# Six places for low parts and four for loads in a Fourier-mixing and attention kernel, with the space taken from the big matrix, and copies that either engine may do

## The chip, the core and the metric

The kernel runs on one core of a Trainium2 chip. The metric is the device time of one execution in microseconds (us): the median of several runs. Beside it one execution is recorded by the hardware profiler; its span is counted from the first instruction to the last.

The core has five engines that matter here: TensorE (PE; its weight loads are listed apart as PEld), ScalarE (ACT), VectorE (DVE), GpSimd (POOL) and SyncE (SP). All transfers between memory and the on-chip buffers are issued from SP's queue. Matrix products go to eight banks of PSUM, from which only ACT and DVE can read here.

## The reference: what is computed

Two independent parts, whose outputs lie side by side (2048 rows of 448 + 448).

```python
# part A: Fourier mixing, S = 2048, D = 448
a = einsum("bsd,ed->bse", x, dft_hid_re);  b = einsum("bsd,ed->bse", x, dft_hid_im)
y = einsum("ts,bse->bte", dft_seq_re, a) - einsum("ts,bse->bte", dft_seq_im, b)
# part B: attention, 16 heads of 28
q, k, v = split(x @ wqkv)
p = softmax(q @ k.T * 28**-0.5);  o = (p @ v) @ wo
out = concatenate([y, o], axis=-1)
```

All is float32. A matrix product that must be precise is made of products of two parts: each operand is split into a high part (rounded to the matmul's format, F32R) and a low part (what is left), and high x high, low x high and high x low are added up in PSUM.

## The kernel before

**A planner writes the order.** The kernel is not written in the order in which it runs. Every piece of work is a task: an engine (or a choice of two, with a price on each), a key, the tasks it depends on, and the buffers it uses. `Schedule.run` (L192) then plays the five engines against each other with the prices given and writes the instructions out: an engine that comes free takes the ready task with the smallest key. A task is ready when its dependencies are done and each buffer it needs has a free place. The result is a fixed order on each engine. So a change of a price, a key or a number of places changes the order of everything behind it.

**Buffers are pools with places** (`Slots`, L100). A place is taken when the first task that uses it is written, and given back when the last one is done. Pools marked "in turn" give their places out in the order of keys. The pools that matter:

- `wraw` (3 places): raw loads, of weights, of folded input rows, and of one in four tiles of the sequence matrix.
- `whi` (3) and `wlo` (4): their high and low parts; `wlo` also holds the differences of three in four sequence tiles.
- `kept` (19 pairs of 512 columns): results on their way out, loads of input rows, intermediate sums, and the exponentials of the attention. A pair for exponentials is only given if one more stays free (`SPARE`).
- `big`: one large tile whose ranges are reused by stage (input of the projections; then the hidden stage's results, the low parts of its tables at 7 S, and at its end, from `TAIL`, the last quarter of the late projection).

**Two streams share TensorE.** One is the attention: for each head and each four key tiles, 16 score matmuls (L1196), 16 exponentials on ACT (L1200), then 32 matmuls for the weighted sum (L1207), which need all 16. The other, called fill, runs in this order:

1. projections of q, k and v (`project`, `values`; matmuls at L573). Their results are split by ACT (L614) and DVE (L615) and stored.
2. the hidden stage of part A, folded by symmetry. `weights_both` adds and subtracts halves of the hidden matrix (L753) and writes tables from the four results (L758 to L766); the tables wait until the projections 1 to 4 are stored, since they lie where those were staged. `rows_both` loads eight pairs of input row tiles (L780), `folded` adds and subtracts their halves into `wraw` (L789), takes half of that as the high part (L791) and the rest as the low part (L792); the matmuls are at L816.
3. the sequence stage, twice (real and imaginary part): `combine` loads and adds the hidden results (L846 to L856), `sequence_halved` loads the sequence matrix (L949), splits a quarter of it (L956, L957), takes differences of the other tiles (L986 to L997) and their largest value (L939), and multiplies (L967).
4. the late projection of the attention's output (`project_late`): three of the four row blocks as soon as heads 0 to 13 are done (loads L1409, splits L1415 and L1417, matmuls L1430), the last block of rows at the end (load L1448, splits L1450 and L1451, two matmuls for each of 16 row groups at L1461). Twelve groups are held on chip in between and added (L1465); the last four stay in their banks and are copied by ACT (L1469) and sent (L1470).

**Keys.** Scores have keys from `T_ATT` to `T_END`, evenly spread over the heads; fill has keys that grow with the planned matmul time, up to `T_FILL`; the last block has `T_OUT` and on. The first keys of a group of heads (`tops`, L1160), from which the rows subtracted before the exponential come, run `LEAD` = 24 ahead of the group's first score. After each head the sums are normalised through memory (`normal`, L1254): copy, store, load, reciprocal, store, load, multiply, store.

## Time and profile before

| | us |
|---|---|
| median of 3 runs | 832.52 (831.48 to 832.91) |
| the profiled execution, its own time | 827.46 |
| its span | 825.6 |
| TensorE busy | 807.9 |
| ACT busy | 619.2 |
| DVE busy | 399.6 |

A row of the groups gives line, engine, operation, what is written from what, the shapes and how many; then busy time in us, the mean of one in ns, and the idle time of the engine just before them with what ended it. Rows of the chain of waits and of the timeline begin with the start and the length in us; "x32" means 32 instructions merged. Buffer names leave out the number of the place. The tile called `wdraw` lies in the same memory as `wd`.

### The profile page before, as it was taken

The numbers are of one execution on the slowest core, as the hardware profiler recorded it, in microseconds if no ns is written. First come the engines' busy times: TensorE is split into PE (matmuls) and PEld (weight loads), VectorE is DVE, ScalarE is ACT, GpSimd is POOL, SyncE is SP. The second block draws the span as 40 slices with busy tenths as digits, with TensorE's granted clock in tenths as the row PEclk, the third lists the DMA queues.
The fourth block names the chain that finished last, engine by engine and source line by source line (L and its number), as shares of the span: only waits on it lengthen the run. The fifth ranks groups of instructions, "written<-read, shape, count | busy, mean of one in ns | idle before, by whom it ended". The sixth has DMA issues, their size and how long they took to land.

```text
span 825.6 us, 14220 instructions
## 1 busy us (share of the span) xinstructions
PE 807.9 (98%) x4872; PEld 524.5 (64%) x4872; DVE 399.6 (48%) x925; ACT 619.2 (75%) x1274; POOL 7.9 (1%) x58
## 2 busy tenths in 40 slices
PE   8999999999999999999999999999999999999994
PEld 7886555755666666657665677656765666655574
DVE  6541324342332335357655378976754476533142
ACT  6207886677888889998777687999777768889731
POOL 3000000000000000000000000000000000000000
PEclk9999999999999999999999999999999999999997
DMA  8747766534423245577646267678766456560143
GB/s 292 229 148 258 213 205 207 200 104 155 133 94 121 74 155 175 174 163 233 207 150 205 69 196 240 209 197 245 218 199 214 143 164 213 156 203 14 34 128 109
DMA packets 136048, 141.28 MB, mean 171 GB/s; under 512 B 36830, under 2 KB 106976, under 8 KB 135968
## 3 DMA queue, kind: packets, MB, share of 16 engines
q1 hardware_dynamic: 135968, 140.29, 55.1%
q8 instruction: 40, 0.66, 0.3%
q14 instruction: 40, 0.33, 0.1%
HBM read 98.82 MB, written 43.12 MB: 172 GB/s over the span
## 4 chain that ended last, share of the span: by engine, by line
PE 93%; DMA 2%; ACT 2%; SPq 1%; DVE 0%; issue 0%; ACTq 0%
PE bank L1196 31%; PE bank L1207 27%; PE bank L573 13%; PE bank L967 12%; PE bank L816 5%; PE bank L1430 3%; ACT kept L1200 1%; PE bank L915 1%; PE bank L1180 1%; DMA kept<-xb 1%; DMA wraw<-wim 1%; DMA kept<-abd 1%; PE bank L1461 1%; PE bank L1287 0%; DMA kept<-ond 0%
## 5 line engine op out<-in xcount | busy, mean ns | idle before, releaser
L1200 ACT ACTIVATE kept<-bank 128x512 f32<-128x512 f32 x1024 | 510.7, 673 | 107.0 <-PE bank L1196 106.2
L1196 PE MATMUL bank<-q,k 85*128 85x512 f32 x1024 | 374.4, 413 | 3.6 <-ACT kept L1200 3.6
L1196 PEld LDWEIGHTS bank<-q,k 85*128 85x128 f32 x1024 | 186.5, 189 | 100.5 <-issue 39.0
L1207 PE MATMUL bank<-kept,v 128*32 128x512 f32 x2048 | 233.9, 597 | 0.0
L1207 PEld LDWEIGHTS bank<-kept,v 128*32 128x32 f32 x2048 | 60.6, 110 | 130.8 <-issue 124.3
L967 PE MATMUL bank<-big,wlo 128*128 128x226 f32 x512 | 106.6, 277 | 0.0
L967 PEld LDWEIGHTS bank<-big,wlo 128*128 128x128 f32 x512 | 96.3, 198 | 9.5 <-issue 0.7
L967 PE MATMUL bank<-big,whi 128*128 128x448 f32 (+1 forms) x256 | 74.6, 323 | 0.0
L573 PE MATMUL bank<-big,whi 128*128 128x512 f32 x196 | 69.6, 398 | 2.3 <-ACT big L512 1.4
L939 DVE TENSOR_REDUCE diff<-wlo 128x1 f32<-128x512 f32 x96 | 65.5, 683 | 2.5
L967 PEld LDWEIGHTS bank<-big,whi 128*128 128x128 f32 x256 | 49.6, 198 | 5.0 <-ACT kept L1200 0.5
L439 DVE COPY kept<-bank 128x226 f32<-128x226 f32 (+4 forms) x63 | 30.3, 502 | 42.5 <-PE bank L816 39.0
L573 PEld LDWEIGHTS bank<-big,whi 128*128 128x128 f32 x196 | 36.8, 189 | 12.5 <-ACT big L512 1.8
L573 PE MATMUL bank<-big,wlo 128*128 128x512 f32 x112 | 44.4, 398 | 0.0
L957 DVE TENSOR_TENSOR wlo<-wraw,whi 128x512 fp32r<-128x512 f32 x32 | 22.0, 688 | 45.2 <-PE bank L967 33.4
L816 PE MATMUL bank<-wd,whi 128*128 128x450 f32 (+3 forms) x128 | 42.7, 369 | 0.0
L573 PE MATMUL bank<-wd,big 128*128 128x448 f32 x176 | 37.6, 370 | 0.0
L1430 PE MATMUL bank<-big 128*128 128x448 f32 x144 | 37.1, 366 | 0.0
L573 PEld LDWEIGHTS bank<-wd,big 128*128 128x128 f32 x176 | 32.8, 188 | 3.9 <-issue 0.7
L986 DVE TENSOR_TENSOR wlo<-wdraw,wraw 128x256 fp32r<-128x256 f32 x64 | 24.4, 423 | 21.5 <-PE bank L967 7.2
L615 DVE TENSOR_TENSOR wd<-bank,wd 128x512 fp32r<-128x512 f32 x16 | 10.8, 686 | 45.4 <-ACT wd L614 43.4
L1260 ACT ACTIVATE kept<-bank 128x512 f32<-128x512 f32 (+1 forms) x19 | 11.5, 606 | 24.0 <-PE bank L1207 24.0
(119 smaller groups left out, 616.9 us busy)
## 6 DMA issues: line engine op xcount, KB each, us to landing
wdraw<-wre SPq DMA_DIRECT2D x48, 256.0 KB
wdraw<-wim SPq DMA_DIRECT2D x48, 256.0 KB
qkd<-wd SPq DMA_DIRECT2D x32, 256.0 KB
q<-qkd SPq DMA_DIRECT2D x64, 112.0 KB
k<-qkd SPq DMA_DIRECT2D x64, 112.0 KB
abd<-kept SPq DMA_DIRECT2D x16, 448.0 KB
kept<-abd SPq DMA_DIRECT2D x16, 448.0 KB
qkd<-kept SPq DMA_DIRECT2D x24, 256.0 KB
```

Of the source, the lines that this page charges most:

```text
L439: nc.vector.tensor_copy(dst, src)
L573: nc.tensor.matmul(o.t[:, :cols], w(), x(), start=(i == 0), stop=(i == n - 1))
L816: nc.tensor.matmul(o.t[:, c0:c1], of(w, i), y(), start=n == 0, stop=n == m)
L939: seen.append(dve(key, lambda: nc.vector.tensor_reduce(dst, f32(flat(src.t)), axis=AX.X, op=ALU.max, apply_absolute_value=True), 0.6, deps ...
L957: b = dve_on(key - 11.5, lambda e: e.tensor_tensor(turned(lo.t), read(same.t), f32(turned(hi.t)), op=ALU.subtract), 0.65, deps=[a], acq=[l ...
L967: nc.tensor.matmul(o.t[:, at0:at0 + n], cut_of(w.t, e, c), x(), start=first, stop=stop)
L986: e.tensor_tensor(turned(dl.t, c, 2, HP), read(r.t, c, 2, HP), read(base.t, c, 2, HP), op=op)
L1196: m = pe(key, lambda e: nc.tensor.matmul(b.t, KT[h][kt // 4].t[:KR + 1, kt % 4 * P:(kt % 4 + 1) * P], q.t[:KR + 1, :], start=True, stop=True),
L1200: return act(key - 20, lambda: nc.scalar.activation(p.t, b.t, AF.Exp, scale=SCALE), deps=[m], use=[b, pair])
L1207: nc.tensor.matmul(o.t[j * VW:(j + 1) * VW, :], VT[h].t[:, kt // 4, kt % 4, :], tiles[i // 2].t[:, i % 2, :], start=(kt < 4 // len(cs)), s ...
L1260: a = act(key - 20, lambda: nc.scalar.activation(osb.t[:n * VW], o.t[:n * VW], AF.Copy, accum_out=sums[:n * VW, g:g + 1]), deps=[dep], use ...
L1430: nc.tensor.matmul(o.t[:, :D], a(), b(), start=(i == 0), stop=(i == 8 and n < N_HELD))
```

## The change

- `wraw` gets a fourth place, `wlo` two more (six). `big` loses 1688 columns behind `TAIL`.
- The low parts of the hidden tables (`low_at`) are no longer in `big`: they take two places of `wlo` for as long as the hidden stage runs.
- The last quarter of the late projection keeps its three high parts in the three places of `whi`, not in `big`.
- Three kinds of copy that only ACT did may be done by ACT or DVE, whichever the planner finds free: the high part of a projection's result (L614), half of the folded rows (L791, "first half"), and the copies of the last four output groups (L1469).
- Each of the last four output groups waits for the end of its own chain of matmuls instead of the end of the last chain.
- Four numbers of the plan: `T_ATT` 24 to 26, `T_END` 666 to 610, `T_FILL` 867 to 926, `T_OUT` 788 to 806.

```diff
-    big = new("big", [P, TAIL + 1736], F32R)
+    big = new("big", [P, TAIL + 48], F32R)
-    wraw = new("wraw", [P, 4, P], F32, 3, True)
+    wraw = new("wraw", [P, 4, P], F32, 4, True)
-    wlo = new("wlo", [P, 4, P], F32R, 4, True)
+    wlo = new("wlo", [P, 4, P], F32R, 6, True)
...
-    T_ATT, T_END, T_FILL, T_OUT = 24.0, 666.0, 867.0, 788.0
+    T_ATT, T_END, T_FILL, T_OUT = 26.0, 610.0, 926.0, 806.0
...
-            a = act(key, lambda o=o, hi=hi: nc.scalar.activation(as_r(hi.t), o.t, AF.Copy), deps=[end], use=[o, *own])
+            a = sch.add({"ACT": ACT_P, "DVE": DVE_P}, key, lambda e, o=o, hi=hi: copy_of(e, as_r(hi.t), o.t), deps=[end], use=[o, *own])
...
-    low_at = [big[:, 7 * S + i * EVEN:7 * S + i * EVEN + (EVEN if i < 2 else ODD)] for i in range(4)]
+    low_in = [wlo.slot() for _ in range(2)]
+
+    def low_at(i):
+        n = EVEN if i < 2 else ODD
+        return flat(low_in[i // 2].t)[:ROWS[i % 2], i % 2 * n:(i % 2 + 1) * n]
...
-        h = act(key + 1, lambda: nc.scalar.activation(hi.t, raw.t, AF.Copy, scale=0.5), ACT_S, deps=d, acq=[hi], use=[raw])
+        def half_of(e):
+            if e == "ACT":
+                nc.scalar.activation(hi.t, raw.t, AF.Copy, scale=0.5)
+            else:
+                nc.vector.tensor_scalar(hi.t, raw.t, 0.5, None, op0=ALU.mult)
+        h = sch.add({"ACT": ACT_S, "DVE": 0.6}, key + 1, half_of, deps=d, acq=[hi], use=[raw])
...
-    mid = [big[:, TAIL + 3 * CH + i * 3 * HT:TAIL + 3 * CH + (i + 1) * 3 * HT] for i in range(2)]
+    mid = [big[:, TAIL + i * 3 * HT:TAIL + (i + 1) * 3 * HT] for i in range(2)]
...
+        last_in = [whi.slot() for _ in range(3)]
+        at_last = lambda c, *ks: [last_in[k] for k in ks if c == 3 and k < 3]
...
         def place_of(c, k):
-            at = 2 * GROUP * (c + 1) + k * CH
-            if c == 3:
-                at = TAIL + k * CH if k < 3 else 2 * GROUP * (k - 2) + 6 * CH
+            if c == 3 and k < 3:
+                return flat(last_in[k].t)
+            at = 2 * GROUP * (c + 1) + k * CH if c < 3 else 2 * GROUP * (k - 2) + 6 * CH
             return big[:, at:at + CH]
...
-                held[n] = o
+                held[n] = o, last[0]
...
-            p = pe(key, emit, n=2, d=M448, deps=[x3_ready[c], *w_ready, *([] if n < N_HELD else [last[0]])], use=[o, x3[c]])
+            p = pe(key, emit, n=2, d=M448, deps=[x3_ready[c], *w_ready, *([] if n < N_HELD else [held[n][1]])], use=[o, x3[c]])
...
-                e = act(key, lambda o=o, pair=pair: nc.scalar.activation(pair.t[:, 0, :D], o.t[:, :D], AF.Copy), 0.43, deps=[p], use=[o, pair])
+                e = sch.add({"ACT": 0.43, "DVE": 0.53}, key, lambda e, o=o, pair=pair: copy_of(e, pair.t[:, 0, :D], o.t[:, :D]), deps=[p], use=[o, pair])
```

More of the change, by code (lines that the diff above doesn't have):

```diff
@@ L760, in weights_both @@
                 ts.append(dve(at, lambda i=i, n=n, pick=pick: nc.vector.tensor_tensor(
-                    halves(low_at[i][:n]), pick(i // 2), halves(f32(table(i, "hi"))), op=ALU.subtract), 0.35, deps=[ts[i // 2]], use=[to]))
+                    halves(low_at(i)), pick(i // 2), halves(f32(table(i, "hi"))), op=ALU.subtract), 0.35, deps=[ts[i // 2]], use=[to, low_in[i // 2]]))
                 for a, op2 in ((0, ALU.subtract), (1, ALU.add)):
@@ L808, in hidden_both @@
                     seq += [(hi, i, lambda i=i: table(i, "main"), 0, 2 * MAIN, M448), (lo, i, lambda i=i: table(i, "hi"), c0, c1, MLOW),
-                            (hi, i, lambda i=i: low_at[i][:ROWS[i % 2]], c0, c1, MLOW)]
+                            (hi, i, lambda i=i: low_at(i), c0, c1, MLOW)]
                 rest = [(hi, i, lambda i=i: table(i, "rest"), 0, 2 * REST, M448) for i in range(4)]
@@ L817, in hidden_both @@
                         last[0] = pe(at, emit, d=d, deps=[last[0], *([h, *ready] if n == 0 else [l] if n == 1 else [])],
-                                     use=[hi, lo, o, *([pair] if n == len(seq) - 1 else [])])
+                                     use=[hi, lo, o, *low_in, *([pair] if n == len(seq) - 1 else [])])
                         at += d
@@ L1415, in project_late @@
                     a = act(key + 2 + i * 36 * M448, lambda raw=raw, i=i, c=c, k=k: nc.scalar.activation(place_of(c, k), raw.t[:, i], AF.Copy), ACT_S,
-                            deps=[ld, free], use=[raw])
+                            deps=[ld, free], use=[raw, *at_last(c, k)])
                     b = dve_on(key + 2 + i * 36 * M448, lambda e, raw=raw, i=i, c=c, k=k: e.tensor_tensor(
-                        place_of(c, 3 + k), raw.t[:, i], f32(place_of(c, k)), op=ALU.subtract), 0.62, deps=[a], use=[raw])
+                        place_of(c, 3 + k), raw.t[:, i], f32(place_of(c, k)), op=ALU.subtract), 0.62, deps=[a], use=[raw, *at_last(c, k)])
                     x[c, k] = [a, b]
@@ L1430, in emit @@
                     nc.tensor.matmul(o.t[:, :D], a(), b(), start=(i == 0), stop=(i == 8 and n < N_HELD))
-                last[0] = pe(key + i * M448, emit, d=M448, deps=[last[0], *x[c, i // 3], *(w_ready if i == 0 else ())], use=[o])
+                last[0] = pe(key + i * M448, emit, d=M448, deps=[last[0], *x[c, i // 3], *(w_ready if i == 0 else ())], use=[o, *at_last(c, 0, 1, 2)])
             if n < N_HELD:
@@ L1456, in project_late @@
             key = T_OUT + n
-            o = bank_s.slot() if n < N_HELD else held[n]
+            o = bank_s.slot() if n < N_HELD else held[n][0]
             def emit(e, n=n, o=o, xt=x3[c], t=t):
```

## The prediction

> **What bounds the kernel now.** I began with the page: busy time of each engine and the costliest groups.
>
> ```profile
> span 825.6 us, 14220 instructions
> PE 807.9 (98%) x4872; PEld 524.5 (64%) x4872; DVE 399.6 (48%) x925; ACT 619.2 (75%) x1274; POOL 7.9 (1%) x58
> L1200 ACT ACTIVATE kept<-bank 128x512 f32<-128x512 f32 x1024 | 510.7, 673 | 107.0 <-PE bank L1196 106.2
> L1196 PE MATMUL bank<-q,k 85*128 85x512 f32 x1024 | 374.4, 413 | 3.6 <-ACT kept L1200 3.6
> ```
>
> TensorE is busy for 98% of the span, so nothing that only moves work between other engines can gain much: what can be won is TensorE's idle time, and what hides inside its busy time. The windows say where the idle time lies (columns: stretch, its length, then busy time of PE, PEld, DVE, ACT, POOL; granted clock, DMA share, GB/s).
>
> ```profile
> 350.00:390.00 40.00, 38.78 (x244) 23.56 (x237) 23.49 (x58) 36.15 (x78) 0.00 (x0) 1.00 0.73 191
> 510.00:550.00 40.00, 39.52 (x244) 25.50 (x242) 34.98 (x86) 39.39 (x90) 0.00 (x0) 1.00 0.69 186
> 550.00:590.00 40.00, 39.21 (x267) 25.61 (x269) 27.24 (x68) 32.81 (x69) 0.00 (x0) 1.00 0.79 243
> 670.00:710.00 40.00, 39.64 (x246) 25.57 (x245) 26.60 (x65) 31.73 (x66) 0.47 (x1) 1.00 0.58 176
> 710.00:750.00 40.00, 39.27 (x232) 21.61 (x231) 15.53 (x34) 33.50 (x69) 0.00 (x0) 0.96 0.51 163
> 806.00:826.00 20.00, 9.15 (x42) 7.55 (x40) 3.35 (x6) 2.52 (x5) 0.00 (x0) 0.77 0.33 112
> ```
>
> The five inner stretches lose 1.22 + 0.48 + 0.79 + 0.36 + 0.73 = 3.6 us, the last one 10.85. The rest of the argument is about three places: the end, a stall near 728, and a hole in the attention near 152 that fixes when the end can begin.
>
> **The end.** Chain of waits (start, length, what), then four rows of the timeline.
>
> ```profile
> 787.31 3.57 PE bank L1207 x32
> ...
> 797.32 4.20 PE bank L1430 x21
> ...
> 810.02 0.45 SPq L1448
> 810.52 3.46 DMA kept<-ond
> ```
>
> ```profile
> 808.37 4.42 PE L1430 MATMUL bank<-big 128*128 128x448 f32 x21
> ...
> 815.46 2.37 PE L1461 MATMUL bank<-big,q 128*128 128x448 f32 x8 [2.67 <-DVE q L1451]
> 816.51 1.89 ACT L1469 ACTIVATE kept<-bank 128x448 f32<-128x448 f32 x4 [1.83 <-PE bank L1461]
> 817.09 2.67 SPq L1470 DMA_DIRECT2D out<-kept  x4
> ```
>
> Two things finish together. The attention's last weighted sum (L1207) ends at 790.9; it is normalised through memory and comes back as the last quarter of the projection's input (L1448) only at 814.0, and the last eight matmuls (L1461) begin at 815.46. From the last L1207 to the end of the span are 825.6 - 790.9 = 34.7 us, whatever else runs. Meanwhile TensorE runs out of fill (the work it does between scores) at 812.79, and waits 2.67. So a faster fill alone gives nothing: the attention must end sooner too.
>
> **The stall near 728.** Timeline and chain of waits:
>
> ```profile
> 727.48 1.10 PE L1196 MATMUL bank<-q,k 85*128 85x512 f32 x3
> 728.82 1.97 PE L1196 MATMUL bank<-q,k 85*128 85x512 f32 x5 [0.24 <-ACT kept L1200]
> 731.27 1.77 PE L1196 MATMUL bank<-q,k 85*128 85x512 f32 x3 [0.49 <-ACT kept L1200]
> 733.70 1.62 SPq L1409 DMA_DIRECT2D kept<-ond  x3
> ```
>
> ```profile
> 695.91 3.81 PE bank L1196 x8
> ...
> 725.19 1.37 PE bank L1196 x5
> ...
> 733.04 4.43 PE bank L1207 x32
> 744.27 3.57 PE bank L1207 x32
> ```
>
> The sequence matmuls (L967) are used up and the late projection (L1430) needs rows of head 13, whose load (L1409) is issued at 733.70. Eleven scores take 733.04 - 727.48 = 5.6 us at the pace of ACT's exponentials, against 1.37/5 = 0.27 us each just before (725.19), 3.0 together: 2.6 lost. The weighted sum behind them takes 4.43 instead of 3.57 while the stretch's clock reads 0.96, another 0.86. Together 3.5 us. The eight scores at 695.91 are the same thing, smaller: 0.48 us each with no fill between them.
>
> The Trainium skill, "Trainium Kernel Development and Optimization", Performance Expectations, says that matmul busy time tells badly how close a kernel is to its limit, since matmuls are pipelined. The row of 710 to 750 agrees: it shows 0.73 us idle where 3.5 are lost. The Trainium skill, "TensorE: Matmul & The Clock Gate", Part 1, has the clock halved after an idle window of some 3.4 us; here it fell behind a stretch in which TensorE was at work about half the time. By the page's rule the 0.86 would not hang on this stall and the sum below would be 0.9 us smaller; by the row it does.
>
> **The hole in the attention.** Chain of waits around 150: starts of the weighted sums of 16 scores each.
>
> ```profile
> 117.30 3.57 PE bank L1207 x32
> 128.20 3.57 PE bank L1207 x32
> 141.22 3.57 PE bank L1207 x32
> 151.10 13.99 PE bank L573 x60
> 166.94 3.57 PE bank L1207 x32
> ```
>
> Periods of 10.9, 13.0 and 25.7 us. In the last, no score runs for 14 us; TensorE does 60 projection matmuls instead. Why not attention? The timeline and the totals of two lines tell:
>
> ```profile
> 143.58 0.74 DVE L789 TENSOR_TENSOR wraw<-kept 128x256 f32<-128x256 f32 x2
> ...
> 158.45 0.76 DVE L789 TENSOR_TENSOR wraw<-kept 128x256 f32<-128x256 f32 x2
> ...
> 162.12 2.48 ACT L758 ACTIVATE wd<-kept 128x226 fp32r<-128x226 f32 x8
> ...
> 164.93 0.63 PE L1196 MATMUL bank<-q,k 85*128 85x512 f32 x2
> ```
>
> ```profile
> L780 SPq DMA_DIRECT2D kept<-xa x8: 393/458/803, 19.4 to 144.9; - x8
> L753 DVE TENSOR_TENSOR kept<-kept,kept x4: 1081/1084/1093, 93.3 to 99.8; 128x896 f32<-128x896 f32 x4
> ```
>
> All draw on the 19 pairs of `kept`. Four sums of the hidden tables (L753) hold a pair each from 94 to 100 on until the tables are written (L758, at 162). Eight loads of input rows (L780) have taken a pair each by 144.9, and give one back only when both their halves have been folded into `wraw` (L789): one has by 150. That is 4 + 7 = 11. A group of 16 scores wants eight pairs and one left over; there are eight. The scores go on at 164.93, when the tables let go. This reading is from the code's rules and these times; the trace doesn't number the pairs.
>
> **The change, part by part.** (1) A fourth place for loads. The fold at 143.58 is the third and the one at 158.45 the fourth; with three places each waits until an earlier one is consumed. With one place more every fold moves one step forward: the fourth to 143.58, and the second input pair is free at about 145 instead of 159. Then the eighth pair is there and the hole closes: 25.7 - 13.0 = 12.7 us, by the period before it. What is late next: the tables still hold four pairs until the fourth projection is stored, and its matmuls now run in the gaps; I charge two periods of 13.0 instead of 10.9, 4.2 us. The attention gains 8.5 us. Bounds: nothing, if the freed pair is taken by a load, and 12.7.
>
> (2) Six low places. Two of them hold the low tables while the hidden stage runs, which leaves the four of before; from the sequence on six serve. DVE waits there for TensorE to free one (below, first row). That costs TensorE only where fill is missing: 3.6 us of idle less the 0.73 counted at 728, and the eight scores at 695.91 that took 3.81 instead of 8 x 0.27 = 2.2, so 2.9 + 1.6 = 4.5 at most. Against it, any new order has stalls of its own of the same size, 4.5 again. I take 0.
>
> ```profile
> DVE wlo L957 <- PE bank L967: 33.4, 15, 5.9
> DVE wd L615 <- ACT wd L614: 43.4, 11, 11.2
> ```
>
> (3) Copies by either engine. DVE stood 43.4 us waiting for ACT's half of the same result (second row) and may now do it itself. Each is one instruction on either side; its cover is DVE's idle half (48% busy). TensorE doesn't wait for it in steady state, so 0; bounds: what the 11 waits could give the hole, already inside (1), and one DVE copy of 0.7 us in the way of a fold.
>
> (4) Places moved. The low tables go from `big` to `wlo`, the last quarter's high parts from `big` to `whi`: the same instructions at other addresses, 0. The last quarter waits for the sequence's last use of `whi`, which its old wait for the last sequence unit covers.
>
> (5) The last four output groups wait for their own chain instead of the last one. If the input is there in time, six of the eight L1461 matmuls run before the end: what follows the last L1430 is two matmuls, one copy, one issue, 0.4 + 0.54 + 0.67 = 1.6 us (4.20/21 = 0.2 a matmul; 1.89 and 2.67 over four), in place of 817.09 + 2.67 - 815.46 = 4.3. Less the six moved ahead, 1.2: 1.5 gained.
>
> (6) Keys. Scores run from 26 to 610 and fill to 926. By 400 us some 476 exponentials have been done (windows of L1200), which is key 24 + 476 x 642/1024 = 322, while the sequence's fill starts at 397 by the code's own formula: scores come first already, and more of that changes nothing. 0; the first keys of a group of heads (24 ahead) move from 38 to 42 scores ahead, 2.6 us for the attention at best.
>
> ```profile
> 0.00:400.00 400.00, 236.45 (x476) 1.00 0.57 177
> ```
>
> **Sum.** With the attention 8.5 us sooner, the stall at 728 goes (3.5), since head 13 is normalised before the sequence ends; so does the wait of 2.67; and 1.5 from (5). For this the last input must be ready 815.46 - (812.79 - 3.5) = 6.2 us sooner; 8.5 is enough. Total 7.7. The profiled run took 827.46 (span 825.6 and 1.9 around it), so 819.8; its time lies 5.1 under the median of 832.52, and I take the difference off the median: **824.8 us**.
>
> **Rivals.** A: the hole stays, as a load takes the freed pair (SP issues the next one at once; for it: eight loads were taken as soon as pairs came free; against: only eight exist). Then the attention's end fixes 34.7 us behind it; at best 2.6 from the keys: 830 to 832.5, I say 831.5. B: everything in (2) is won too: 824.8 - 4.5 = 820.3. C, slower: pairs run out again later, where the loads for combining (L846, two pairs a group) sit nearer together as fill keys stretch to 926. A second hole of 12.7 behind the middle, less the 8.5 won: the attention ends 4.2 later, 836.7; it decides as soon as its length passes 8.5 us. For it: the pool is at its limit at 150; against: the chain has no second piece like that of 151.10.
>
> **Numbers.** Forecast 50%, its own range 821.5 to 829; A 20%, B 15%, C 15%. A tenth of a percent or two can't be told from no change here, so 0.2% is the bound: under 830.85 is faster, over 834.2 slower. Faster: the forecast, B, and a quarter of A, 0.70; same 0.15; slower 0.15. The range reaches B's side to 818 and A's to 834.5.
>
> **What would show it.** Right: no period over 14 us between weighted sums up to 210; the L758 tables later than 162 while scores run; PE at 39.9 or more in 710 to 750 with clock 1.00; the L1448 load of the last quarter issued before 804; L1470 copies spread out, not four together behind the last L1461. Wrong: the 14 us hole again (A), or the last L1207 ending after 790.9 (C). If the hole is gone and the end is not sooner, my claim that the attention's end sets the time fails.

## The result, and the profile after

The changed kernel takes 818.47 us (median of five runs, 817.08 to 818.62), the kernel before 831.67 (831.36 to 832.91) beside it: a ratio of 0.9827, 95% interval 0.9807 to 0.9848. It is faster, by 13.2 us where 7.7 were forecast: 3.0 us below the forecast's own range (821.5 to 829), and 0.5 above the lower end of the wide one (818). The profiled execution took 817.08 us, its span 815.3. From the page:

```profile
span 815.3 us, 14231 instructions
PE 803.5 (99%) x4872; PEld 525.5 (64%) x4872; DVE 416.9 (51%) x956; ACT 604.4 (74%) x1243; POOL 7.8 (1%) x58
L1209 ACT ACTIVATE kept<-bank 128x512 f32<-128x512 f32 x1024 | 511.1, 674 | 125.6 <-PE bank L1205 125.6
L1205 PE MATMUL bank<-q,k 85*128 85x512 f32 x1024 | 371.1, 411 | 0.8 <-ACT kept L1209 0.7
```

The lines of the kernel have moved: exponentials are at L1209, scores at L1205, weighted sums at L1216, sequence matmuls at L976, the late projection at L1441, its last matmuls at L1472. TensorE's matmuls are as many as before; they fill 4.4 us less, and scores wait 0.7 us for exponentials where they waited 3.6. The windows (columns as in the prediction):

```profile
350.00:390.00 40.00, 39.20 (x240) 22.45 (x236) 17.47 (x41) 40.00 (x89) 0.00 (x0) 1.00 0.66 166
510.00:550.00 40.00, 40.00 (x277) 26.35 (x276) 29.32 (x71) 32.20 (x70) 0.00 (x0) 1.00 0.71 229
550.00:590.00 40.00, 39.02 (x224) 22.99 (x223) 27.64 (x71) 38.28 (x85) 0.00 (x0) 0.96 0.70 185
670.00:710.00 40.00, 40.00 (x274) 26.25 (x274) 24.71 (x60) 28.96 (x60) 0.00 (x0) 1.00 0.58 177
710.00:750.00 40.00, 40.00 (x254) 26.67 (x252) 20.13 (x51) 33.95 (x71) 0.47 (x1) 1.00 0.48 144
```

The stall near 728 is gone (40.00 at clock 1.00); one like it, clock 0.96 and 0.98 us idle, now stands in 550 to 590. The end, by the chain of waits:

```profile
773.55 3.57 PE bank L1216 x32
777.12 1.41 PE bank L1472 x6
...
795.00 7.21 PE bank L1441 x36
802.22 0.40 PE bank L1472 x2
802.62 1.20 PE bank L1441 x6
803.82 0.40 PE bank L1472 x2
...
808.25 0.41 PE bank L1472 x2
808.66 0.02 issue
808.68 0.54 ACT kept L437
```

and by SP's timeline:

```profile
795.28 1.09 SPq L1459 DMA_DIRECT2D kept<-ond  x2
...
803.23 6.36 SPq L1481 DMA_DIRECT2D out<-kept  x4
```

The last weighted sum ends at 777.12 instead of 790.88. The last quarter's input is loaded from 795.28 on (810.02 before), so nothing waits for it: TensorE multiplies without a gap until 808.66, with the last output groups between the fill. The end is no longer set by the attention. Then the hole, by the chain of waits, DVE's timeline (folds) and ACT's (tables):

```profile
115.40 3.57 PE bank L1216 x32
...
126.18 3.57 PE bank L1216 x32
...
142.67 3.57 PE bank L1216 x32
...
155.53 3.57 PE bank L1216 x32
...
164.79 5.04 PE bank L573 x22
...
171.69 3.55 PE bank L1216 x29
```

```profile
139.44 0.40 DVE L793 TENSOR_TENSOR wraw<-kept 128x256 f32<-128x256 f32 x1
...
156.85 0.75 DVE L793 TENSOR_TENSOR wraw<-kept 128x256 f32<-128x256 f32 x2
```

```profile
166.81 1.95 ACT L762 ACTIVATE wd<-kept 128x226 fp32r<-128x226 f32 x6
```

The fourth fold comes at 139.44 (158.45 before) and the scores get on sooner, but not at their usual pace: periods of 16.5, 12.9 and 16.2 us where there were 13.0, 25.7 and 11.5. The ninth weighted sum starts at 171.7 instead of 178.5.

**A measure for TensorE.** Busy time hides waiting (a score that follows a waiting score counts as busy). So I add up, over all matmuls, the time from one start to the next, less what a matmul of that shape needs when nothing holds it up: the lower quartile for its shape in all twenty profiles (0.233 us for a score, 0.107 for one of 226 columns), and for the weighted sums 3.57/32 = 0.1116. What is over is "lost". Since the matmuls are the same in all the kernels, the lost time alone makes their spans differ, but for the few us behind the last matmul. By stretches, in us of the profiled executions, with the weighted sums as marks:

| kernel | median us | last weighted sum ends | from there to the end | lost to 24th | 24th to 32nd | 32nd to 56th | 56th to last matmul | lost in all |
|---|---|---|---|---|---|---|---|---|
| before | 831.67 | 790.9 | 34.7 | 13.6 | 7.2 | 19.2 | 14.1 | 54.1 |
| changed | 818.47 | 777.1 | 38.2 | 11.5 | 5.5 | 19.0 | 9.1 | 45.1 |
| raw3 | 832.06 | 793.9 | 35.3 | 13.2 | 9.8 | 18.6 | 15.7 | 57.3 |
| keys_old | 833.17 | 797.2 | 35.3 | 12.9 | 11.0 | 19.1 | 18.3 | 61.4 |
| act_copies | 830.06 | 795.8 | 38.5 | 11.6 | 21.0 | 22.1 | 9.5 | 64.3 |
| lo4 | 827.26 | 787.1 | 37.2 | 11.2 | 9.8 | 22.5 | 10.2 | 53.7 |
| half_act | 825.60 | 786.1 | 38.3 | 13.9 | 12.1 | 19.1 | 9.2 | 54.3 |
| places_only | 831.27 | 792.4 | 37.4 | 12.1 | 14.1 | 19.8 | 13.7 | 59.7 |
| keys_only | 832.46 | 794.4 | 34.8 | 13.6 | 7.2 | 19.6 | 18.5 | 58.9 |
| copies_only | 841.81 | 807.7 | 34.3 | 15.3 | 16.3 | 23.1 | 16.0 | 70.7 |
| rows_held | 848.32 | 776.5 | 69.5 | 16.6 | 7.2 | 29.0 | 22.8 | 75.7 |
| rows_held_after | 828.42 | 768.3 | 59.1 | 11.1 | 3.2 | 25.6 | 17.6 | 57.5 |
| edge_after | 818.83 | 778.4 | 38.2 | 11.0 | 6.7 | 19.6 | 9.4 | 46.7 |
| edge_half | 817.19 | 778.0 | 36.8 | 11.1 | 6.4 | 16.8 | 10.2 | 44.5 |
| edge_copies | 827.01 | 788.2 | 36.2 | 11.2 | 9.3 | 22.9 | 10.8 | 54.2 |
| edge_raw3 | 826.44 | 792.2 | 34.9 | 13.6 | 4.3 | 21.9 | 15.6 | 55.4 |
| edge_keys | 824.26 | 789.8 | 35.3 | 14.8 | 5.0 | 17.5 | 15.6 | 53.0 |

A profiled execution is one of many: that of act_copies took 836.17 us, 6 above its median, so its columns are too high by about that. Columns are for finding the place, medians for the price. From before to changed the span is 10.3 us shorter: 2.1 + 1.7 + 0.2 + 5.0 = 9.0 lost time, and 1.1 behind the last matmul (7.77 to 6.64). Two things can be read off the table. The hole costs TensorE next to nothing: between the first and the 12th sum, where it lies, 3.8 us are lost before, 3.5 in raw3, which has it again, and 3.4 in the changed kernel; the rest of the 2.1 lies ahead of the first sum (5.5 against 4.0) and behind the 12th. And the stretch from the 24th to the 32nd sum, where the hidden stage hands over to the sequence stage, differs most from kernel to kernel.

**What the table doesn't tell apart: the clock.** By the windows the granted clock is 1.00 or 0.50, and 0.50 for 3.4 us at a time or two or three times that. This row of half_act, taken just behind a wait, is one of them:

```profile
400.60:407.43 6.83, 6.46 (x21) 5.66 (x22) 5.51 (x16) 3.97 (x8) 0.00 (x0) 0.50 1.08 302
```

Between the first full clock and the last matmul the clock is at 0.50 for 3.4 us in the changed kernel and 4.6 in the kernel before, but for 10.2 in raw3, lo4, edge_after and edge_copies, 13.7 in half_act, 20.5 in places_only and both kernels with held rows, 23.9 in act_copies and keys_old, 27.3 in copies_only. At half the clock up to half of the time is lost, so by estimate up to 10 of the 19.2 us that act_copies loses more than the changed kernel are clock, not waits. These stretches don't hang on the order alone: fill930, whose matmuls stand in the changed kernel's order, has 6.8 us of them. That is one more reason to take prices from medians.

### The profile page after: what moved, and what is told of

Same layout as the page of the kernel before. It is cut to its first block, busy times and chain, and to the rows that moved or that the text cites. A ratio compares the mean times of both kernels' runs of the same rounds, so it can differ in the third digit from the quotient of the medians.

```text
span 815.3 us, 14231 instructions
## 1 busy us (share of the span) xinstructions
PE 803.5 (99%) x4872; PEld 525.5 (64%) x4872; DVE 416.9 (51%) x956; ACT 604.4 (74%) x1243; POOL 7.8 (1%) x58
## 4 chain that ended last, share of the span: by engine, by line
PE 94%; ACT 2%; DMA 1%; DVE 1%; SPq 0%; issue 0%; DVEq 0%
PE bank L1205 31%; PE bank L1216 27%; PE bank L573 13%; PE bank L976 12%; PE bank L825 5%; PE bank L1441 4%; ACT kept L1209 2%; PE bank L924 1%; PE bank L1472 1%; PE bank L1189 1%; DMA kept<-xb 1%; DMA kept<-abd 1%; PE bank L1296 0%; DVE big L865 0%; DVE kept L862 0%
## 5 line engine op out<-in xcount | busy, mean ns | idle before, releaser
L1209 ACT ACTIVATE kept<-bank 128x512 f32<-128x512 f32 x1024 | 511.1, 674 | 125.6 <-PE bank L1205 125.6
L1205 PE MATMUL bank<-q,k 85*128 85x512 f32 x1024 | 371.1, 411 | 0.8 <-ACT kept L1209 0.7
L1205 PEld LDWEIGHTS bank<-q,k 85*128 85x128 f32 x1024 | 186.8, 189 | 91.5 <-issue 38.0
L1216 PE MATMUL bank<-kept,v 128*32 128x512 f32 x2048 | 234.2, 598 | 0.0
L1216 PEld LDWEIGHTS bank<-kept,v 128*32 128x32 f32 x2048 | 60.5, 110 | 131.1 <-issue 124.7
L976 PE MATMUL bank<-big,wlo 128*128 128x226 f32 x512 | 107.2, 276 | 1.0 <-DVE wlo L1003 1.0
L976 PEld LDWEIGHTS bank<-big,wlo 128*128 128x128 f32 x512 | 97.9, 198 | 10.5 <-DVE wlo L1003 1.2
L976 PE MATMUL bank<-big,whi 128*128 128x448 f32 (+1 forms) x256 | 76.1, 324 | 0.0
L976 PEld LDWEIGHTS bank<-big,whi 128*128 128x128 f32 x256 | 49.4, 198 | 5.4 <-ACT kept L1209 0.6
L999 DVE TENSOR_TENSOR wlo<-wdraw,wraw 128x508 fp32r<-128x508 f32 x32 | 21.9, 685 | 53.6 <-PE bank L976 51.0
L573 PEld LDWEIGHTS bank<-big,whi 128*128 128x128 f32 x196 | 36.9, 189 | 10.8 <-DVE big L433 1.7
L1269 ACT ACTIVATE kept<-bank 128x512 f32<-128x512 f32 (+1 forms) x19 | 11.6, 608 | 30.9 <-PE bank L1216 29.0
L1192 DVE STREAM_TRANSPOSE kept<-bank 128x512 f32<-128x512 f32 (+1 forms) x20 | 14.2, 710 | 36.6 <-PE bank L1189 36.5
L1441 PE MATMUL bank<-big 128*128 128x448 f32 x120 | 29.1, 365 | 0.0
```

Of the source, the lines that this page charges most:

```text
L573: nc.tensor.matmul(o.t[:, :cols], w(), x(), start=(i == 0), stop=(i == n - 1))
L976: nc.tensor.matmul(o.t[:, at0:at0 + n], cut_of(w.t, e, c), x(), start=first, stop=stop)
L999: e.tensor_tensor(turned(dl.t, 1, 1, P - 1), mirror(r.t), read(base.t, 1, 1, P - 1), op=minus)
L1192: r = dve(key, lambda o=o, mt=mt: nc.vector.transpose(mt.t[:32 * n, 0], o.t[:32 * n]), 0.64, deps=[m], acq=[mt], use=[o], own=RAW_S)
L1205: m = pe(key, lambda e: nc.tensor.matmul(b.t, KT[h][kt // 4].t[:KR + 1, kt % 4 * P:(kt % 4 + 1) * P], q.t[:KR + 1, :], start=True, stop=True),
L1209: return act(key - 20, lambda: nc.scalar.activation(p.t, b.t, AF.Exp, scale=SCALE), deps=[m], use=[b, pair])
```

## The experiments

The theories: P, the freed pair and the hole (the prediction); K, the four numbers; C, the copies; L, that any other order is as good or bad by accident; S, that the parts need each other. Later ones are told where they arise.

**Parts undone, one at a time.** Three load places instead of four:

```diff
-    wraw = new("wraw", [P, 4, P], F32, 4, True)
+    wraw = new("wraw", [P, 4, P], F32, 3, True)
```

> The changed kernel with three places for loads again (wraw), all else as changed. Theory P (pairs: the fourth place moves each fold of input rows one step forward, so that a pair of kept is free when the attention near 150 us needs it): the first fold is back at about 88 us, a stretch of 10 us or more without a score is back before 170 us, the last weighted sum ends 5 us or more later than 777, and the time is 3 to 8 us above the changed kernel. Theory K (the new keys of the plan carry the gain, the places little): within 2 us of the changed kernel. Theory L (any new order of this planner differs by some us, in either direction): anything within 4 us, without the hole.

832.06 us, 1.0021 [1.0003, 1.0039] of before: the whole gain is gone. The hole is back (chain of waits):

```profile
141.72 3.57 PE bank L1216 x32
...
151.82 12.83 PE bank L573 x56
...
166.63 3.57 PE bank L1216 x32
```

The fourth place is what shortens the hole. But 13.6 us are more than theory P's 3 to 8, so something else is lost with it.

The old four numbers (24, 666, 867, 788) in the changed kernel:

> The changed kernel with the four old numbers of the plan (24, 666, 867, 788). Theory P: within 2 us of the changed kernel, since scores came first already. Theory K: most of the gain is lost, 6 to 12 us slower. Theory L: anything within 4 us.

833.17 us, 1.0016 [0.9996, 1.0036]. All three kinds of copy on ACT only, in the changed kernel:

```diff
-            a = sch.add({"ACT": ACT_P, "DVE": DVE_P}, key, lambda e, o=o, hi=hi: copy_of(e, as_r(hi.t), o.t), deps=[end], use=[o, *own])
+            a = sch.add({"ACT": ACT_P}, key, lambda e, o=o, hi=hi: copy_of(e, as_r(hi.t), o.t), deps=[end], use=[o, *own])
...
-        h = sch.add({"ACT": ACT_S, "DVE": 0.6}, key + 1, half_of, deps=d, acq=[hi], use=[raw])
+        h = sch.add({"ACT": ACT_S}, key + 1, half_of, deps=d, acq=[hi], use=[raw])
```

(and in the same way at L1480).

> The changed kernel with the three kinds of copies on ACT alone again. Theory P: 0 to 2 us slower, the copies were hidden; the hole stays as small as in the changed kernel. A rival, theory C (copies: the projections' results reach memory sooner when DVE copies them, and that is what makes the attention earlier): the last weighted sum 5 us or more later, 4 us or more slower. Theory K: no difference. Theory L: anything within 4 us.

830.06 us, 0.9982 [0.9965, 0.9998]. Four low places instead of six (two of them still hold the tables during the hidden stage):

```diff
-    wlo = new("wlo", [P, 4, P], F32R, 6, True)
+    wlo = new("wlo", [P, 4, P], F32R, 4, True)
```

> The changed kernel with four places for low parts, two of which hold the tables in the hidden stage. Theory P: the sequence stage loses what two more places gave, which I had put at nothing against 4.5 us at most, and the hidden stage has two places left for folded rows: 1 to 6 us slower, with more of DVE's waits for TensorE in the sequence stage. Theory K: within 2 us. Theory L: anything within 4 us.

827.26 us, 0.9962 [0.9944, 0.9980]. So each of four parts, undone alone, costs 9 to 15 us, more than theory P had for any of them. Together that is 48.7 us, nearly four times the gain, so these prices don't add up. (lo4 takes two places from the hidden stage as well, so it undoes more than the two new ones.) The old dependence of the last four groups:

```diff
-deps=[x3_ready[c], *w_ready, *([] if n < N_HELD else [held[n][1]])]
+deps=[x3_ready[c], *w_ready, *([] if n < N_HELD else [last[0]])]
```

> The changed kernel in which the last four output groups wait again for the end of the last chain. TensorE's order differs only there, so this is the one part that can be undone by itself: the prediction said 1.5 us, with all eight last matmuls behind the last L1441 again and four copies in a row. Theory L expects that too, as the order before 780 us stays. 1 to 2.5 us slower.

819.19 us, 0.9861 [0.9836, 0.9887]: 0.7 us slower where 1 to 2.5 were expected, which these runs don't tell from nothing.

**Is it an accident of the order?** `T_END` 612 for 610, and `T_FILL` 930 for 926, each alone:

> The changed kernel with T_END 612 in place of 610, a change of a third of a percent in the scores' keys that nothing should feel. Theory L (the size of the gain is that of one lucky order: each undone part cost 9 to 15 us, far more than the parts can be worth one by one): 4 us or more slower than the changed kernel, the loss between 360 and 420 us, where the sequence stage takes over. Theory S (the parts need each other: with all of them in, the gain is there whatever the keys): within 2 us.

> The changed kernel with T_FILL 930 in place of 926. Theory L: 4 us or more slower, again lost between 360 and 420 us or in one other place; the stretch around 150 us as in the changed kernel, since the fourth place for loads is there. Theory S: within 2 us.

821.57 us, 0.9905 [0.9876, 0.9934], and 818.47 us, 0.9867 [0.9833, 0.9902]. The second tells nothing of orders: its TensorE order is the changed kernel's, matmul for matmul. The first has 694 of the 4872 matmuls at another place in the order and costs 3.1 us, between theory S's 2 and theory L's 4; 9.6 us are lost between its 24th and 32nd sum instead of 5.5, where theory L had put it. So one other order costs 3 us, not 10: theory L in its strong form isn't borne out, but one order is a small sample.

**Parts alone, in the kernel before.** The new places (and the last groups' own chains) alone, the new numbers alone, the copies alone:

> The kernel before with the new places alone (four load places, six low places, tables and last quarter moved, own chain of the last groups), its copies on ACT and its four numbers left as they were. Theory S (the parts need each other: whichever single one was undone in the changed kernel cost 9 to 15 us, so none alone carries the gain): 829 to 834 us, the hole at 150 shorter than before (a period of 16 to 20 us instead of 25.7) but what is won there lost by 420 us. Theory P (the freed pair is the whole cause): the hole shorter and the gain kept, 820 to 826 us, last weighted sum ending by 783.

> The kernel before with the four new numbers (26, 610, 926, 806) alone. Theory S: 829 to 836 us; the hole at 150 stays at 24 to 26 us, since the pairs are as few as before. Theory K (the new numbers carry the gain, as undoing them cost 15 us): 820 to 826 us. The prediction had 2.6 us at best for them, 830.

> The kernel before with the three kinds of copy by either engine alone. Theory S: 829 to 835 us, the hole at 150 stays at 23 to 26 us. Theory C (the copies carry the gain, as undoing them cost 12 us): 820 to 826 us. The prediction had 0 for them.

831.27 us, 0.9993 [0.9974, 1.0011]; 832.46 us, 1.0003 [0.9988, 1.0018]; 841.81 us, 1.0109 [1.0076, 1.0141]. No part gains alone, and the copies alone lose 10, which theory S (829 to 835) had not expected either. Theories P, K and C fall as single causes; S is left, with that miss. The table shows where places_only loses what it wins: its hole is nearly as short as in the changed kernel (17.5, 12.9 and 17.6 us), then 14.1 us go in the handover, by the same estimate up to 5.1 of them for 10.2 us at clock 0.50.

**Does the attention's end set the time?** In the kernel before, the loads of input rows are held back until their key comes near, so that they don't take pairs early:

```diff
-        return x, dma(key, put, 128, n=5, use=[x])
+        return x, dma(key, put, 128, n=5, hold=True, use=[x])
```

> The kernel before, with one change: the eight loads of input rows of the hidden stage are held until the fill has come near to their keys, so that they don't take pairs of kept early. Theory P: the hole of 14 us near 152 goes (no period over 14 us between weighted sums up to 210), the weighted sum of group 8 begins 8 to 12 us sooner than 178. The time then depends on what follows: if the attention's end sets the time, as the prediction said, 5 to 10 us faster; if orders after it differ by luck, anywhere from 10 faster to the same. A rival to P (the hole comes from the projections, whose results the next head needs): the hole stays.

848.32 us, 1.0240 [1.0176, 1.0305]. The hole is gone altogether (periods of 11.0, 11.9, 11.0), the attention ends at 776.5, as soon as in the changed kernel, and the time is 17 us longer. TensorE's timeline behind the attention:

```profile
786.09 0.74 PE L967 MATMUL bank<-big,wlo 128*128 128x226 f32 x4 [2.89 <-DVE wlo L997]
787.55 1.20 PE L967 MATMUL bank<-big,wlo 128*128 128x226 f32 x4 [0.72 <-DVE wlo L997]
793.84 0.93 PE L967 MATMUL bank<-big,whi 128*128 128x448 f32 x2 [5.09 <-ACT whi L956]
```

The projections that used to fill the hole have become sequence work left over at the end, where no score covers the wait for DVE and ACT. The same edit in the changed kernel (the text below speaks of the kernel before with the four new numbers; what was run has the whole change and the held loads):

> The kernel before with its row loads held back (848.3 us: hole gone, attention 14 us sooner, TensorE short of fill at 783 to 794) and the four new numbers beside it, which put fill further back against the scores. Theory T (the time is TensorE's work plus what it loses, and scores pulled ahead of the fill only leave fill behind that waits for DVE): as slow or slower, 845 to 855 us, with TensorE busy for 12 us or less in a stretch of 20 behind the attention's end. Rival (the attention's end sets the time): 820 to 830 us.

828.42 us, 0.9960 [0.9936, 0.9983]. It lies in the rival's range, but as the kernel is another than the one forecast, its number decides neither for theory T nor for the rival. What it shows is this: the edit closes the hole in the changed kernel too (periods of 10.6, 11.5, 11.0 and 9.9), and costs 10 us there. The attention ends at 768.3, sooner than in any other kernel, and 59.1 us follow it: the end of the attention does not set this time. Closing the hole entirely is no gain; the fill must be done when the attention is.

**The handover.** What is lost there? The changed kernel with the fold's half alone on ACT (the middle edit of the copies above):

> The changed kernel with only the half of the input fold (two of the four steps between load and low part) back on ACT; the projection's copy and the last output copy stay with either engine. If the cost of undoing all three copies (11.6 us) hangs on the fold's chain, 826 to 831 us with a period of 16 us or more near 360 to 410; if on the projection's copy, 818 to 821. Theory L (any other order of the same work is as good or bad by chance): anywhere between 818 and 833, with the loss in a place that has nothing to do with the fold.

825.60 us, 0.9928 [0.9906, 0.9950]. It is 0.4 us below what was expected if the fold's chain is what counts (826 to 831). It follows the changed kernel, some 2.5 us behind (lost at the start, where its clock reads 0.50 from 11.5 to 14.9 us), up to 392 us; then TensorE stands. Timeline of TensorE, then of SP's queue, then the chain of waits:

```profile
395.97 1.20 PE L1205 MATMUL bank<-q,k 85*128 85x512 f32 x4
399.25 0.62 PE L976 MATMUL bank<-big,wlo 128*128 128x226 f32 x3 [2.09 <-DVE wlo L1003]
...
400.97 0.56 PE L976 MATMUL bank<-big,wlo 128*128 128x226 f32 x1 [0.76 <-DVE wlo L1003]
```

```profile
384.34 0.87 SPq L958 DMA_DIRECT2D wdraw<-wre  x1
385.26 0.64 SPq L901 DMA_DIRECT2D edge<-wre  x1
385.94 6.47 SPq L898 DMA_DIRECT2D edge<-wre  x3
392.46 2.75 SPq L958 DMA_DIRECT2D wdraw<-wre  x2
```

```profile
392.46 4.35 DMA wdraw<-wre
396.83 0.76 DVE wlo L995 x2
...
398.46 0.60 DVE wlo L999
```

Four small loads (L901, L898: single columns of the sequence matrix, for the edges of its tiles) hold SP for 7.1 us. The sequence's own operands (L958) go only at 392.46, land 4.35 us later, and DVE's differences come too late. The order on TensorE is fixed, so the scores behind the waiting L976 stand as well. Theory H: the loss in the handover is this, and how much of it shows depends on when these loads go and how soon behind them TensorE's order needs the operands. The first four of them (for the real part) need not wait for the hidden stage:

```diff
+        early = after if part else [ab_done[0]]
...
-            edge[:, i], src[NT - 2 * i, :, :, 0]), 64, extra=4.0, deps=after) for i in range(1, 4)]
+            edge[:, i], src[NT - 2 * i, :, :, 0]), 64, extra=4.0, deps=early) for i in range(1, 4)]
...
-        ld = dma(key, lambda: nc.sync.dma_start(raw, src[HT, :, :, 0]), 64, extra=4.0, deps=after)
+        ld = dma(key, lambda: nc.sync.dma_start(raw, src[HT, :, :, 0]), 64, extra=4.0, deps=early)
```

(what is written from them into `big` still waits). This edit in three kernels: half_act, act_copies and the changed one.

> The kernel with the fold's half on ACT alone (825.6 us, which stands 2.09 and 0.76 us before a sequence matmul near 397) with one more edit: the four small loads of edge columns for the sequence's first part (7.1 us of SP's time there, 385.3 to 392.4, with the sequence's own operand loads queued behind) may go as soon as the hidden stage has stored its first result. Theory H (TensorE's loss at the handover is late operand loads behind these four): 818 to 821 us, no wait of TensorE for DVE's wlo near 397. Rival L (the loss there changes with any order of the same work): anywhere from 818 to 833 with a stall of another cause between 350 and 420.

> The same edit in the kernel with all three kinds of copy on ACT alone (830.1 us; it loses some 15 us more than the changed kernel between its 24th and 32nd weighted sum; its edge loads hold SP for 3.3 us). Theory H: the loss falls by the 3 us that SP is freed and what they made late, 822 to 828 us. Rival: the loss there comes from the pairs of kept that the loads for combining wait for, and not from the edge loads: 828 to 832 us with the same long period of 18 us.

> The same edit in the changed kernel. TensorE doesn't wait for a load at the handover there (no idle time from 385.11 on), so theory H gives nothing or little: 816 to 820 us. Rival L: anywhere from 816 to 833, with new stalls in the handover.

817.19 us, 0.9839 [0.9803, 0.9875], 8.4 less than without the edit; 827.01 us, 0.9945 [0.9924, 0.9965], 3.1 less; 818.83 us, 0.9849 [0.9819, 0.9879], the same. In edge_half the loads go at 227 to 238 us (SP's timeline):

```profile
226.98 0.61 SPq L902 DMA_DIRECT2D edge<-wre  x1
234.53 3.79 SPq L899 DMA_DIRECT2D edge<-wre  x3
```

and TensorE's row of the windows around the handover, half_act first:

```profile
320.00:420.00 100.00, 96.65 (x587) 59.45 (x586) 47.06 (x111) 89.42 (x191) 0.00 (x0) 0.97 0.65 182
```

```profile
320.00:420.00 100.00, 99.75 (x625) 62.08 (x618) 52.08 (x120) 92.11 (x199) 0.00 (x0) 0.98 0.60 186
```

edge_half came 0.8 us below theory H's range, the other two lie inside theirs, though the intervals of edge_copies and act_copies touch. Of edge_half's gain the table puts 5.7 us in the handover, where the waits for DVE are gone; 2.8 more lie ahead of the 24th sum, nearly all in the first 75 us, before any of these loads goes in either kernel. Up to 385.7 us its TensorE order is half_act's, behind that it differs, so a part may be the new order's. It also shows that the fold's half by either engine is worth nothing by itself: with the loads out of the way it doesn't matter (817.19 and 818.83). In other kernels theory H isn't the whole of the handover: in keys_old TensorE waits 2.1 us there, for ACT and not for these operands, and in places_only for nothing longer than 0.5.

**What the parts are worth with the handover cleared.** Theory E: two separate causes, the attention's end and the handover. Three load places, and the old numbers, each in edge_after:

> The changed kernel with its edge columns loaded early (818.8 us) and three load places instead of four: the part of the fourth place by itself, the handover's late loads out of the way. Theory E (two separate causes: the attention's end, which the hole makes late, and the handover's late loads): the hole's period is 24 to 26 us again, the last weighted sum ends at 787 to 791, the last 34 to 36 us follow it whatever the fill does, TensorE waits 2 to 3 us before its last matmuls: 824 to 828 us. Theory H alone (the handover is all): 818 to 821 us, the hole costs nothing as TensorE works through it.

> The changed kernel with its edge columns loaded early (818.8 us) and the four old numbers (24, 666, 867, 788): the part of the keys by itself. Theory E: the last weighted sum ends at 787 to 793 since the scores are spaced for a later end, the last 34 to 36 us follow it: 823 to 829 us. Theory H alone: 818 to 821 us.

826.44 us, 0.9937 [0.9921, 0.9954], 7.6 above edge_after; 824.26 us, 0.9904 [0.9882, 0.9925], 5.4 above it. In edge_raw3 the two places of the prediction are back, to a hundredth of a us in length. Timeline of TensorE:

```profile
728.59 1.97 PE L1206 MATMUL bank<-q,k 85*128 85x512 f32 x5 [0.24 <-ACT kept L1210]
731.04 1.77 PE L1206 MATMUL bank<-q,k 85*128 85x512 f32 x3 [0.48 <-ACT kept L1210]
...
817.00 1.88 PE L1473 MATMUL bank<-big,q 128*128 128x448 f32 x8 [2.67 <-DVE q L1463]
```

Its last weighted sum ends at 792.2, 1.2 us later than expected, and 34.9 us follow. Theory E holds for both. It doesn't for the copies: edge_copies' last sum ends late too (788.2), but 36.2 us follow it and only 10.8 are lost behind its 56th sum; 5.9 of the 7.5 us that it loses more than edge_after lie between the 24th and the 56th sum. Why is open. None of these versions is faster than the changed kernel by more than the runs can tell.

## Why the prediction was wrong, and where it was right

The direction and the mechanism of the end were right; the size was not: 818.47 us are 6.3 under the forecast. Two steps of the prediction failed.

**The first failed step: from profile to median.** "Its time lies 5.1 under the median ..., and I take the difference off the median": the changed kernel's profiled execution lies 1.4 under its median, so 3.7 of the 6.3 us are this step. The profiled execution of before (827.46, granted clock 0.993) was quicker than all 83 executions beside the later runs, which took 828.1 to 835.9 at clocks of 0.984 to 0.993, only two of them at 0.993. So the offset was that of one lucky execution, not a property of the kernel.

**The second: (3) copies and (6) keys at 0, and each part priced alone.** The other 2.7 are the profiled times' difference, 827.46 - 817.08 = 10.4, against the sum of 7.7. The sum had a gain only at the end, and there it had too much: 5.0 of lost time and 1.1 behind the last matmul, 6.1 for what was forecast as 3.5 + 2.67 + 1.5. But 2.1 us were won up to the 24th sum and 1.7 in the handover, for which it had nothing. The reasons given, that the copies are hidden and that the keys change nothing, were read off the kernel before. For the numbers that holds there (keys_only, 832.46); the copies alone cost 10 there; the low places (2) were not run alone. In the changed kernel undoing the numbers costs 5.4 us and the copies 8.2 (827.01 against 818.83), both with the handover cleared, and the low places 8.8 (4.5 was the bound), without that: 4.3 of it in the handover, 4.6 behind. The numbers, the copies and the fourth place are each needed for the attention to end before 780; with any of them undone and the handover cleared it ends at 788 to 792. So adding up prices of parts, each taken in the kernel before, is what failed. Which part won the 2.1 and the 1.7 stays open.

**The end: right.** It said that the last weighted sum fixes the last 34.7 us. In before, raw3, keys_old, keys_only, copies_only, edge_raw3 and edge_keys 34.3 to 35.3 us follow it, whether it ends at 790 or 808, and 14 to 18.5 us are lost behind the 56th sum. In the changed kernel and most of the rest 36 to 39 follow, with 9 to 11 lost. rows_held sets the limit: a sooner end helps only as long as the fill is done as well. That was a rival I hadn't named.

**(1) The fourth place: right in kind, wrong in shape.** The fold moved as said (139.44; 143.58 forecast), the tables came later than 162 (166.81). The hole did not close: two periods over 14 us (16.5 and 16.2), so that sign failed. I had charged 4.2 us for the tables' pairs; 45.5 us for the three periods against 50.3, with the 2.0 from sooner, make 6.8 won by the ninth sum where I had 8.5. The attention ended 13.8 us sooner, so 7.0 came later, for which I had no step; they weren't needed, as 6.2 are enough. The price, with the handover cleared, is 7.6 us, against the 6.2 of stall (3.5) and wait (2.67) that hang on it in the sum. Those two come and go together, in edge_raw3 as in the kernel before.

**The handover: missed.** No step had it. It lost 7.2 us before and 5.5 in the changed kernel, a gain of 1.7 only, but up to 21 in kernels with a part undone. In the changed kernel the edge loads go from 379.0 to 385.5 and hold SP for 4.9 us of it; the sequence's own loads go on behind them at 385.52, 7 us sooner than in half_act (SP's timeline):

```profile
379.71 2.59 SPq L898 DMA_DIRECT2D edge<-wre  x1
...
385.52 2.78 SPq L958 DMA_DIRECT2D wdraw<-wre  x3
```

Its first L976 starts at 385.11, that of half_act at 387.21, neither after a wait; the operands of the next ones are there in time in the changed kernel, and the edit that cures half_act changes nothing. The order alone doesn't settle it: last_chain, whose TensorE order is the same up to 802 us, waited 1.23 us for ACT at 398. Why this order comes out so, and that of places_only doesn't, I can't derive from the edits; it stays open, and in this narrow sense theory L holds.

**(5) Own chains: 1.5 forecast.** The copies are spread (L1481 from 803.23), and 1.1 us less lie behind the last matmul. That can't be put down to the chains: undone alone they cost 0.7, within the scatter, and keys_only, which has the old ones, has 6.6 us there as well. (In that step's sum one copy is 1.89/4 = 0.47, not 0.54, which changes the 1.5 by less than 0.1.)

**Rivals.** A didn't come (the hole shrank), nor C (no second hole). B's number, 820.3, is the nearest, but by luck, not for its reason: from the 32nd to the 56th sum 19.0 us are lost instead of 19.2, as "a new order has stalls of its own" had it, among them the one in 550 to 590. There TensorE waits 0.98 us at 574.2 for DVE's operands, behind the second four edge loads (558.0 to 564.3), which no run moved.

## What to carry to other kernels

Where two streams share an engine, price a change by the engine's lost time and by which stream ends last, not by a hole in one stream: a hole that the other stream fills costs nothing by itself, and closing it can cost more than it gave. Parts that are worth nothing alone may each be needed for the last stream to stop being last, so undoing one at a time doesn't add up. Where one engine's order is fixed, look at what lies in the load queue ahead of the first operands of each new stage. And don't carry one profiled execution's distance from the median over to another kernel.

## What the runs showed of the hardware

An issue's time doesn't follow its size. In half_act the four loads of 8 KB took SP 0.64 to 3.1 us each, and one took 4.41 in copies_only, while loads of 256 KB on the same queue took 0.38 to 0.47 where nothing held them up. The transfers of half_act from 385.0 to 392.5 us (packets, then the queue's packets, MB and share of 16 engines' time):

```profile
DMA packets 5909, 0.77 MB, mean 102 GB/s; under 512 B 5370, under 2 KB 5908, under 8 KB 5908
...
q1 hardware_dynamic: 5908, 0.76, 68.7%
```

The engines are busy for 68.7% of the time with 0.77 MB, in pieces nearly all under 512 bytes. The Trainium skill, "Perfetto Trace Analysis", What "DMA-bound" means, counts the issuing engine's queue as a limit of its own, whose time goes into writing out a transfer's pieces, not into moving data; the trace agrees in so far as SP took 7.1 us for 32 KB. Whether it was writing pieces or waited for room in the queue was not separated. And the clock fell again with little idle time: the 0.96 of the changed kernel in 550 to 590 is 0.50 from 579.1 to 582.5, with 0.98 us idle in all the 40 us and none in the 3.4 us just before, in which eight matmuls ran. The Trainium skill, "TensorE: Matmul & The Clock Gate", Part 1, has it fall after an idle window of some 3.4 us; the trace shows no such window. What sets the fall off here no run shows.
